# Inverting 32x32 blocks unit by unit, with the rows dealt to four partitions

## The chip, the cores and the metric

The kernel runs on one core of a Trainium2 chip. The metric is the device time of one execution in microseconds (us). "Before" and "after" are the two kernels. Every run lists the span of its profiled execution and the mean granted clock of TensorE. Runs that were timed in rounds are compared with runs of the kernel before on the same chip in the same session; their fast runs lie within about 1.2% of each other for before and 0.4% for the others. Runs of different sessions and chips are also set side by side below; the median of before in these sessions lies between 980.35 and 985.25 us, so a difference of a few microseconds between two sessions means little.

Names of engines: PE is TensorE (PEld its weight loads), DVE VectorE, ACT ScalarE, POOL GpSimd, SP SyncE, which issues transfers.

## The reference, cut to what matters

```python
# q, k, v: (4, 8, 768, 48), beta: (4, 8, 768); w_in: (384, 2048), w_out: (2048, 384), float64
k_n = k / (np.linalg.norm(k, axis=-1, keepdims=True) + 1e-06)
for t in range(S):                       # a recurrence over 768 positions
    y[t]  = q[t] . state
    state = state + beta[t] * outer(k_n[t], v[t] - state . k_n[t])
x = y as (3072 tokens, 384)
h = x @ w_in
out = (h * np.cos(h)) @ w_out            # the FFN
```

The kernels take 64 positions of two batch entries (16 heads) as one **unit**; there are 24 units. Inside a unit the recurrence is a triangular system, whose 64x64 matrices are inverted by halves: two 32x32 triangular blocks by elimination on GpSimd, the rest by matmuls.

## The kernel before

A unit passes four stages, each a generator whose parts are merged with those of other units: `prepare` (norm of k, transposes, Gram matrix), `invert`, `complete` (the other half of the inverse) and `recur` (the recurrence); every two units feed one pass of `ffn`.

```python
def prepare(n):
    nc.scalar.square(ksq, kd)
    nc.vector.tensor_reduce(out=ksum, in_=ksq, ...)
    nc.gpsimd.tensor_tensor(out=knrm, in0=ksum, in1=halves, op=ALU.pow)
    nc.vector.tensor_scalar_add(knrm, knrm, 1e-6)
    nc.vector.reciprocal(krec, knrm)
    nc.gpsimd.tensor_tensor(out=kd, in0=kd, in1=krec..., op=ALU.mult)
    yield
    # ... transposes p_t, copied to kq_t by ScalarE; then the Gram matrix p_g
    nc.scalar.copy(by_parity(g), p_g[:, :, :, 0])
    nc.sync.dma_start(out=g_dr, in_=g)            # through DRAM into gb,
    # ... four units of a group side by side in gb's 128 partitions
    yield

def invert(gr):                                   # four units at once, 6 times
    nc.gpsimd.tensor_tensor(out=a, in0=a, in1=bb[...], op=ALU.mult)   # beta
    # ... clear y, write the diagonal
    for j in range(HC - 1):                       # 31 steps
        shape = [128, j + 1, HC - 1 - j]
        nc.gpsimd.tensor_tensor(out=part, in0=y[:, 0:j+1, j, None]..., in1=a[:, j, None, j+1:]..., op=ALU.mult)
        nc.gpsimd.tensor_tensor(out=behind, in0=behind, in1=part, op=ALU.subtract)
        if j % 5 == 4:
            yield
    nc.sync.dma_start(out=y_drs[gr], in_=yb)      # out to DRAM; complete() reads it back as yt
    yield

def ffn(p):
    for f in range(0, FT, 2):
        # p_h = w_in . x                          TensorE
        # turns <- p_h (ScalarE); r (VectorE, twice); abs, sin of r (ScalarE, twice)
        nc.vector.tensor_tensor(out=gs[-1]..., in0=r, in1=p_h, op=ALU.mult)   # g_ffn
        yield
```

The float64 weights are narrowed to float32 in the kernel, by eight VectorE passes and one GpSimd addition per tile (28 tiles), merged into the first steps.

## Time and profile before

| | before |
|---|---|
| time, median of the first 3 runs | 984.12 us (983.04 to 989.65) |
| span of the profiled run, granted clock | 985.7 us, 0.955 |
| TensorE busy | 775.6 us (79%) |
| VectorE, ScalarE, GpSimd busy | 418.8, 288.7, 336.7 us |
| first 188 us: TensorE busy | 50.1 us |
| units 4 to 20 | 34.2 us per unit, 28.0 to 32.9 in undisturbed steps |

The table reads like this: TensorE has the most work and is idle mainly in two places, the beginning and the six times when GpSimd inverts four units. The prediction below shows the lines.

### The profile page before, as it was taken

To read this page: it belongs to the slowest core of one execution; us is meant where nothing else is said; L and a number is where in the kernel's file an instruction comes from. 1 tells how busy PE (TensorE), PEld (TensorE's weight loads), DVE (VectorE), ACT (ScalarE), POOL (GpSimd) and SP (SyncE) were. 2 spreads that over 40 slices of the span, in tenths; PEclk is the share of its full clock that TensorE was granted. 3 is DMA by queue.
4 is the path that set the end of the run, shared out by engine and by line. 5 is a ranking of instruction groups with operands and counts; after the bars stand their busy time and mean duration, and the time that the engine had idled before them with its cause. 6 is when DMAs were issued, how large, how long until landed. Compare 5 with 4: busy or idle time off the path is not lost. (4 is left out here: it accounts for less than half of the span.)

```text
span 985.7 us, 19148 instructions
## 1 busy us (share of the span) xinstructions
PE 775.6 (79%) x8136; PEld 568.0 (58%) x8136; DVE 418.8 (42%) x772; ACT 288.7 (29%) x530; POOL 336.7 (34%) x481
## 2 busy tenths in 40 slices
PE   0600026729699996899997999988999979999997
PEld 0400025627377674577674686665776847768674
DVE  2586796564235153053262152342441622605141
ACT  1300002124135242044251163341442512515241
POOL 4459734248600159210188011295001850000000
PEclk9999999779799998899998899998999998999999
DMA  6461351540221220231321222303312021000000
GB/s 129 98 191 49 103 130 52 120 88 2 80 51 42 53 55 9 76 66 26 69 40 33 66 53 62 71 2 84 66 25 60 10 78 39 4 18 2 9 9 16
DMA packets 140950, 55.05 MB, mean 56 GB/s; under 512 B 130113, under 2 KB 133441, under 8 KB 140097
## 3 DMA queue, kind: packets, MB, share of 16 engines
q1 hardware_dynamic: 139968, 53.73, 22.5%
q8 instruction: 64, 1.05, 0.5%
q10 hardware_dynamic: 896, 0.10, 0.1%
q14 instruction: 22, 0.17, 0.1%
HBM read 36.41 MB, written 17.40 MB: 55 GB/s over the span
## 5 line engine op out<-in xcount | busy, mean ns | idle before, releaser
L500 PE MATMUL p_o<-w_out,g_ffn 128*128 128x384 f32 x768 | 292.9, 521 | 13.9 <-DVE g_ffn L492 13.3
L471 PE MATMUL p_h<-x_ffn,w_in 128*128 128x256 f32 x1152 | 276.2, 388 | 24.4 <-DVE g_ffn L492 24.2
L471 PEld LDWEIGHTS p_h<-x_ffn,w_in 128*128 128x128 f32 x1152 | 215.4, 192 | 65.5 <-DVE g_ffn L492 17.9
L500 PEld LDWEIGHTS p_o<-w_out,g_ffn 128*128 128x128 f32 x768 | 144.3, 199 | 100.0 <-DVE g_ffn L492 16.8
L243 POOL TENSOR_TENSOR knrm<-ksum,halves 128x8 f32<-128x8 f32 x24 | 40.7, 1697 | 252.9 <-DVE ksum L239 241.2
L328 POOL TENSOR_TENSOR yb<-yb,part 128x31 f32<-128x31 f32 (+15 forms) x186 | 111.1, 597 | 14.0
L492 DVE TENSOR_TENSOR g_ffn<-r,p_h 128x512 f32<-128x512 f32 x96 | 65.8, 685 | 113.8 <-ACT r L489 113.8
L321 POOL TENSOR_TENSOR part<-yb,gb 128x31 f32<-128x31 f32 (+15 forms) x186 | 103.0, 554 | 13.8
L488 ACT ACTIVATE r<-r 128x512 f32<-128x512 f32 x96 | 60.7, 632 | 160.4 <-DVE r L485 160.4
L357 PE MATMUL p_w<-yt,gc 64*64 64x32 f32 x768 | 33.0, 230 | 87.5 <-DMA yt<-y_dr 87.3
L482 DVE SCALAR_TENSOR_TENSOR r<-turns,p_h 128x512 f32<-128x512 int32 x96 | 65.7, 684 | 82.5 <-ACT turns L480 81.8
L357 PEld LDWEIGHTS p_w<-yt,gc 64*64 64x64 f32 x768 | 29.7, 147 | 98.9 <-DMA yt<-y_dr 76.2
L485 DVE SCALAR_TENSOR_TENSOR r<-turns,r 128x512 f32<-128x512 int32 x96 | 75.4, 786 | 2.3
L480 ACT ACTIVATE turns<-p_h 128x512 int32<-128x512 f32 x96 | 57.0, 594 | 61.2 <-PE p_h L471 51.1
L489 ACT ACTIVATE r<-r,halfpi 128x512 f32<-128x512 f32 x96 | 69.5, 724 | 2.6
L279 DVE TENSOR_TENSOR tt<-p_g,masks 128x256 f32<-128x256 f32 x48 | 18.2, 418 | 86.6 <-ACT gc L276 86.6
L258 ACT COPY kq_t<-p_t 128x512 f32<-128x512 f32 x48 | 28.1, 586 | 69.4 <-PE p_t L257 69.3
L417 PE MATMUL p_u<-rhs,yt 64*64 64x48 f32 x704 | 29.6, 230 | 17.3 <-DVE rhs L406 17.3
L307 POOL TENSOR_TENSOR gb<-gb,bb 128x1024 f32<-128x1024 f32 x6 | 14.4, 2400 | 81.6 <-DMA gb<-g_dr 64.1
L510 ACT COPY o<-p_o 128x384 f32<-128x384 f32 x24 | 11.5, 480 | 102.8 <-PE p_o L500 102.8
L371 PEld LDWEIGHTS p_x<-wt,yq 64*64 64x64 f32 x768 | 26.9, 145 | 24.4 <-DVE wt L361 12.7
L417 PEld LDWEIGHTS p_u<-rhs,yt 64*64 64x64 f32 x704 | 25.7, 143 | 26.4 <-DVE rhs L406 19.5
(61 smaller groups left out, 693.8 us busy)
## 6 DMA issues: line engine op xcount, KB each, us to landing
y_dr<-yb SPq DMA_DIRECT2D x6, 1040.0 KB
pairs<-in_moe_w_in_dram SPq DMA_DIRECT2D x12, 512.0 KB
g_dr<-g SPq DMA_DIRECT2D x24, 256.0 KB
pairs<-in_moe_w_out_dram SPq DMA_DIRECT2D x16, 384.0 KB
yt<-y_dr SPq DMA_DIRECT2D x96, 64.0 KB
kp<-in_k_dram SPq DMA_DIRECT2D x48, 96.0 KB
qp<-in_q_dram SPq DMA_DIRECT2D x48, 96.0 KB
vp<-in_v_dram SPq DMA_DIRECT2D x48, 96.0 KB
```

The costliest lines, as they stand in the source:

```text
L321: nc.gpsimd.tensor_tensor(out=part, in0=y[:, 0 : j + 1, j, None].to_broadcast(shape), in1=a[:, j, None, j + 1 :].to_broadcast(shape), op=A ...
L328: nc.gpsimd.tensor_tensor(out=behind, in0=behind, in1=part, op=ALU.subtract)
L357: nc.tensor.matmul(p_w[half(i), h], gc[half(i), h * HC : h * HC + C], yt[half(i), h, HC:C])
L417: nc.tensor.matmul(p_u[half(i), h], yt[half(i), h], rhs[half(i), h])
L471: nc.tensor.matmul(p_h[:, i], w_in[:, t, (f + i) * 128 : (f + i + 1) * 128], x[:, t], start=(t == 0), stop=(t == KT - 1),)
L480: nc.scalar.activation(turns, p_h, AF.Copy, scale=1.0 / (2.0 * math.pi))
L482: nc.vector.scalar_tensor_tensor(out=r, in0=turns, scalar=-PI2_HI, in1=p_h, op0=ALU.mult, op1=ALU.add)
L485: nc.vector.scalar_tensor_tensor(out=r, in0=turns, scalar=-PI2_LO, in1=r, op0=ALU.mult, op1=ALU.add)
L488: nc.scalar.activation(r, r, AF.Abs)
L489: nc.scalar.activation(r, r, AF.Sin, bias=halfpi, scale=-1.0)
L492: nc.vector.tensor_tensor(out=gs[-1][:, f % 4 : f % 4 + 2], in0=r, in1=p_h, op=ALU.mult)
L500: nc.tensor.matmul(p_o, gs[f // 4][:, f % 4, i * 128 : (i + 1) * 128], w_out[:, f], start=(f == 0), stop=(f == FT - 1),)
```

## The change

Its intent: invert each unit by itself, with a quarter of every block's rows on each of four partitions, so that no four units wait for one long inversion and the first inversion is ready early; take the multiplication by beta off GpSimd by putting it into the evictions of g and u, which then move from ScalarE to VectorE; and narrow the weights with three VectorE passes instead of eight. The core of the diff (cuts marked `...`):

```diff
 def prepare(n):
     ...
-    g = work.tile([128, H, C], FP, name="g", bufs=1)
-    nc.scalar.copy(by_parity(g), p_g[:, :, :, 0])
+    g = work.tile([128, H, C], FP, name="g")
+    for par in range(2):
+        nc.vector.tensor_tensor(out=g[:, par::2], in0=p_g[:, par, :, 0], in1=bt[:, n, par::2, None]..., op=ALU.mult)
     ...
-    nc.sync.dma_start(out=g_dr, in_=g)            # and four reads into a quarter of gb
+    for y in range(4):
+        nc.sync.dma_start(out=g_dr[y]..., in_=g[y * HC : (y + 1) * HC, ...])
+    for y in range(4):                            # each block read to four sets of partitions
+        nc.sync.dma_start(out=gb[n][y * HC : (y + 1) * HC]..., in_=g_dr[y]...[None].to_broadcast([SPLIT, H, HC * HC]))
-def invert(gr):
-    nc.gpsimd.tensor_tensor(out=a, in0=a, in1=bb[...], op=ALU.mult)
-    nc.gpsimd.memset(y, 0.0)
+def invert(n):
+    buf = zb[n % 2]
+    nc.scalar.copy(z, eye)                        # the identity, dealt to four partitions
     for j in range(HC - 1):
-        shape = [128, j + 1, HC - 1 - j]
+        rows = j // SPLIT + 1
+        shape = [128, rows, HC - 1 - j]
         ... the same multiply and subtract on GpSimd
-    nc.sync.dma_start(out=y_drs[gr], in_=yb)
+    for y in range(4):
+        nc.sync.dma_start(out=z_drs[n][y]..., in_=buf[y * HC : (y + 1) * HC, ...])
 def recur(n):
-    nc.scalar.copy(u, p_u)
+    nc.vector.tensor_tensor(out=u, in0=p_u, in1=bt[:, n, :, None]..., op=ALU.mult)
 def narrow(dst, src, n):
-    ... eight VectorE passes, one GpSimd addition
+    nc.scalar.activation(t1.bitcast(FP), hi.bitcast(FP), AF.Abs)
+    ... three VectorE passes
+    nc.scalar.activation(t2, lo, AF.Copy, scale=2.0**-29)
+    nc.gpsimd.tensor_tensor(out=w, in0=w, in1=t2, op=ALU.add)
 # step n of the main loop
+    prepare(n + 3), complete(n + 1), recur(n), invert(n + 2), ffn((n - 2) // 2) by halves
```

The norm (knrm and the product kp) stays on GpSimd, as before.

Names used below: g is the Gram matrix times beta, g_dr its copy in DRAM, and gb that copy spread over the partitions for the inversion. zb is the inverse in the making; it goes through z_dr in DRAM to yt, and yq is yt transposed. ksq, ksum, knrm and kp lead from k to its normalised form. Names with p_ are results of matmuls; each lies in a bank, one of the kernel's few buffers for results, and TensorE writes the next one there only when other engines have read it (mostly copying it out, an eviction; in after p_h waits 57.5 us in all for g_ffn). turns, r, g_ffn, p_h and p_o belong to the FFN.

## The prediction

> **What bounds the kernel now.** I read the page first, then the chain of waits in order of time, then stretches of the span, then the times at which one per-unit instruction recurs, then GpSimd by shape. First the page:
>
> ```profile
> span 985.7 us, 19148 instructions
> PE 775.6 (79%) x8136; PEld 568.0 (58%) x8136; DVE 418.8 (42%) x772; ACT 288.7 (29%) x530; POOL 336.7 (34%) x481
> PE   0600026729699996899997999988999979999997
> POOL 4459734248600159210188011295001850000000
> PEclk9999999779799998899998899998999998999999
> ```
>
> TensorE has the work, but not evenly. Its slices are almost empty for the first seven (some 190 us), and later each dip (0, 6, 7) follows a burst of GpSimd (88, 295, 185): the block inversion, done for four units at once. The stretches say the same in us (PE, PEld, DVE, ACT, POOL busy; granted clock; DMA share; GB/s):
>
> ```profile
> 0.00:188.00 188.00, 50.09 (x652) 41.22 (x652) 124.95 (x248) 22.53 (x50) 100.70 (x121) 0.98 0.44 112
> 188.00:280.00 92.00, 66.38 (x675) 47.99 (x674) 39.81 (x76) 23.04 (x40) 51.90 (x76) 0.82 0.21 51
> 345.00:420.00 75.00, 62.49 (x618) 44.76 (x618) 24.74 (x43) 19.73 (x34) 43.33 (x69) 0.89 0.20 46
> 500.00:560.00 60.00, 51.55 (x448) 34.47 (x447) 18.49 (x33) 14.62 (x26) 37.34 (x59) 0.89 0.14 38
> 850.00:936.00 86.00, 86.00 (x833) 61.09 (x832) 27.25 (x47) 27.43 (x46) 0.00 (x0) 1.00 0.03 8
> ```
>
> In the first 188 us TensorE is busy 50; VectorE has 125 and GpSimd 101. Around each group boundary TensorE is idle 8 to 26 us and its clock falls to 0.82 to 0.89; at 850 to 936, with nothing to invert, it is full and at 1.00. How a boundary stalls, in the chain:
>
> ```profile
> 750.80 3.27 issue
> 754.67 2.01 DMA g_dr<-g
> 757.82 2.42 DMA gb<-g_dr
> 760.44 2.36 POOL gb L307
> 802.93 4.35 DMA y_dr<-yb
> 807.72 2.00 DMA yt<-y_dr
> 809.86 0.39 PE p_w L357 x2
> ```
>
> From 760.4 to 802.6 there is only GpSimd (62 multiply and subtract instructions, 39.7 us); then a transfer out, one in, and p_w of the first unit. Four units wait for this one end. What an undisturbed unit costs I take from the starts of the matmuls p_kq (one group per unit):
>
> ```profile
> 283.78 1.15 PE L396 MATMUL p_kq<-st,kq_t 48*64 48x48 f32 x64
> 316.72 1.15 PE L396 MATMUL p_kq<-st,kq_t 48*64 48x48 f32 x64
> 423.53 1.15 PE L396 MATMUL p_kq<-st,kq_t 48*64 48x48 f32 x64
> 562.44 1.15 PE L396 MATMUL p_kq<-st,kq_t 48*64 48x48 f32 x64
> 697.25 1.15 PE L396 MATMUL p_kq<-st,kq_t 48*64 48x48 f32 x64
> ```
>
> These are units 4, 5, 8, 12 and 16; unit 20 starts at 830.3 and unit 23 at 914.0 in the chain. Units 4 to 20 take 546.5 us for 16: 34.2 each. Clean steps are 32.9 with two prepares in the step (283.8 to 316.7) and 28.0 with none (830.3 to 914.0 is 83.7 for 3). So a prepare costs 2.4 and a step with one prepare is 30.4 us.
>
> [...] The trace: 31 elements take 0.25 us and 255 take 0.66 in quiet places, 1.83 ns per element and 0.19 us fixed; start to start there is 0.075 more. So small instructions are mostly fixed cost. [...] among subtracts of 0.6 us single ones take 1.0, eight such within the 40 us above. [...] 0.82 in the stretch with 25.6 us of idle, 1.00 in full ones. [...] the trace has 0.42 us for a tensor_scalar over 512 words and 0.69 for two-input ones.
>
> **The change part by part.**
>
> GpSimd. Before: per group 62 instructions on sum((j+1)(31-j)) = 5456 elements for each of the two kinds; 62 x 0.19 + 2 x 5456 x 0.00183 = 31.8 us clean, 35.7 measured (214.1 busy / 6), 39.7 with gaps. After: a block's 32 rows lie on four partitions, so step j covers j//4+1 rows; the sum is 1560. Clean 62 x 0.19 + 2 x 1560 x 0.00183 = 17.5; gaps 62 x 0.075 = 4.7; contention some 2.5 (eight events of 0.35 in 40 us, scaled to a step of 30). That is about 25 us per unit, 24 times: 600 us in place of 6 x 41. The elements fall by 3.5 per inversion but the instructions are four times as many in all. The beta product (6 x 2.40) and the clearing (6 x 0.96) leave GpSimd. With knrm 1.7, kp 0.9 and the VectorE gap between them 0.7, GpSimd has 28.3 us per step against TensorE's 30.4: it keeps up, with 2 us to spare.
>
> Order. Unit n+2 is inverted in step n and completed in step n+1. GpSimd is in order, so knrm of the next prepare waits behind the inversion, and TensorE meets p_t of that prepare a quarter into its step: the slack is some 5 us, not a whole step.
>
> Narrowing. The eight VectorE passes cost 18.3+13.8+13.0+12.3+22.2+20.7+18.8+16.8 = 135.9 us. After there are three: (0.47+0.59+0.89) x 12 + (0.47+0.61+0.62) x 16 = 51 us. ScalarE gets 28 x 2 x 0.6 = 34 us, in a stretch where it is 12% busy. GpSimd's add stays (37 us).
>
> Evictions with beta. g and u move from ScalarE (0.58, 0.48) to VectorE (2 x 0.42, about 0.5). VectorE then has per step 4 x 2.16 of FFN and about 6 of the rest, half of 30.4. u now queues behind g_ffn, perhaps 1 us later; rhs has always done so and hardly made TensorE wait after 280 except at boundaries.
>
> Transfers. The 128 B pieces move from the read of gb to the write of g_dr, the 256 B pieces from the read of yt to the write of z_dr: the same number per unit. gb grows from 128 to 512 KB per unit, 9 MB more of 55 at an average DMA share of 22%. No gain or loss.
>
> The beginning. The 16 beta transfers hold ScalarE's queue to 12.9 us; four now end near 3. My estimate: first k at 5, knrm to 8, kp at 9.5, two transposes and p_g by 16, g by 18, through DRAM (two trips of about 4, with the weights beside them) by 27; the weight adds ahead on GpSimd make it 30. Inversion 0: 22 + 5 adds of 1.4 = 28 (to 58). Inversion 1: 3.3 + 23 + adds 8.3 = 35 (to 93). Inversions 2 and 3: 3.3 + 23 + 4.2 each (to 124 and 154). The FFN begins in step 2, whose p_t needs inversion 3 done plus 3.3: 157. That point is a quarter into the step, so p_kq of unit 2 starts near 151 and unit 4's at 151 + 60.8 = 212, in place of 283.8: gain 72.
>
> The middle. Units 4 to 20: 16 x 30.4 = 486 in place of 546.5: gain 60. Units 20 to 23: 30.4 + 28 + 28 = 86.4 in place of 83.7: loss 2.7. From 914.0 to the end, 71.7, is the same work. Sum: 985.7 - 72 - 60 + 2.7 = 856 of span; the timed median lies 1.6 under the span: **855 us**.
>
> **The rivals.** (a) GpSimd becomes the bound: 1536 more instructions in its chain, four times as many as before, and 28.3 against 30.4 is a thin margin. If an instruction costs 0.05 more than I take, the step is 31.4 and the time some 875; at 33 us, inversion 23 ends at 154 + 20 x 33 = 814, its p_kq comes some 20 later, and 72 more make 906. For: the fixed cost dominates and contention now meets every step. Against: the measured small instructions (0.25 to 0.33). (b) The start is bound by transfers: g_dr sits behind up to eight weight loads of 512 KB instead of five, on one queue. The DMA share is 0.44 in the first 188 us, which speaks against, but first landings of 10 to 20 us more would give 865 to 875. (c) The middle gains nothing because TensorE waits for VectorE instead: u, g and FFN in one line. Against: 42% busy, and full TensorE at 850 to 936. Each microsecond of stall per unit would add 20: 875. (d) Better than I think: if the inversions start at 22 and the adds hide, 835.
>
> **Range and chances.** The sum is 855. Rivals (a) to (c) each pull by about 20 and are not exclusive; (d) pulls by 20 the other way. I take 828 to 888. To be within 2% of before all of the middle and most of the beginning would have to fail: 3%; slower 2%; faster 95%.
>
> **What would show it.** Right: p_w for the first time near 65 instead of 124; p_kq of unit 4 near 212; even steps of 30 to 31 with granted clock near 1.00 and no dips in the slices; GpSimd at 60 to 70% with an inversion of 62 instructions in 22 to 26 us; VectorE down by some 60 in all. Wrong: p_t or knrm waiting for GpSimd in every step (a); gb landing after 40 (b); p_s waiting for u (c); steps of 33 or more.

0.82 and 1.00 are granted clocks. The "contention" of 2.5 us is the estimate from eight slow instructions in the inversion from 762.9 to 802.9 (five subtracts, three multiplies: 0.71 to 1.22 us, where their neighbours of like size take 0.37 to 0.72). Each of them ran while VectorE made its second pass over r (L485); what slows them, no run shows. And "in order": in after the power to knrm, its input ready at 519.1, starts at 528.14, when the inversion ahead of it has ended.

## More of the kernel before

Where one execution only was made ("one look"), its state is unknown, and only differences of many microseconds are read from it.

## The result, and the profile after

After takes 1073.95 us, median of 4 runs (1071.79 to 1074.3), beside 983.58 of before (978.35 to 989.65, 4 runs). The ratio is 1.0912, 95% interval 1.0847 to 1.0977: 9% slower. (Ratios here are the mean time of one kernel's fast runs over that of the other's in the same rounds, so not quite the quotient of the medians.) The result is correct.

The page of after, the lines that answer to those of before:

```profile
span 1072.4 us, 20510 instructions
PE 811.3 (76%) x8184; PEld 598.7 (56%) x8184; DVE 356.6 (33%) x706; ACT 300.7 (28%) x562; POOL 531.7 (50%) x1579
PE   4123156579797697698698697698697996998998
POOL 3686767675354644644644644644644553460000
PEclk9999997688898898898898898898898998998999
```

The deep dips of before are gone, but a shallow one comes back in every third slice: TensorE never fills, and its clock stays at 0.8 to 0.9 (0.909 in the mean of the span). GpSimd has no bursts and is about half busy in the middle. Nothing is full. The stretches (columns: PE, PEld, DVE, ACT, POOL busy; granted clock; DMA share; GB/s):

```profile
345.00:420.00 75.00, 60.27 (x614) 43.78 (x613) 24.80 (x51) 21.41 (x40) 39.96 (x124) 0.87 0.22 48
500.00:560.00 60.00, 50.24 (x571) 38.37 (x570) 22.81 (x43) 20.26 (x36) 31.34 (x99) 0.91 0.22 50
850.00:936.00 86.00, 76.17 (x821) 55.30 (x820) 30.03 (x56) 24.52 (x47) 37.20 (x125) 0.92 0.20 46
```

In the last of them before had 86.00 of 86.00 at full clock. In after TensorE has 76.17. So the loss shows as waiting, everywhere alike; a smaller part, as the pair of steps below shows, is that matmuls take longer where the granted clock is lower. I put the starts of p_kq, the first recurrence matmul of a unit, side by side (us from the span's start, from the timelines; the kernels of the last three columns come below):

```
unit      before   predicted   after    e6     e13    e15
2            197         151     146   157     141    119
4            284         212     255   260     237    217
5            317         242     305   291     268    254
20           830         698     902   748     725    711
23           914         785     999   832     809    795
span         986         856    1072   905     880    867
4 to 20     34.2        30.4    40.4  30.5    30.5    30.9  per unit
```

After loses 43 us against the prediction by unit 4, 160 from unit 4 to 20 (16 times 10), 11 to unit 23 and 1 behind it: with rounding 216, the whole of 1072 - 856. Most steps alternate between 38 and 42 us.

**One pair of steps.** From the timeline of after (start, duration, engine, line, operation; in brackets the idle time of the engine before it and what ended it). The inversion that began at 504.26 ends at 528.2; this is what stands around its end:

```profile
518.55 0.55 DVE L253 TENSOR_REDUCE ksum<-ksq 128x8 f32<-128x384 f32 x1
519.33 0.72 ACT L508 ACTIVATE r<-r,halfpi 128x512 f32<-128x512 f32 x1
527.98 0.21 POOL L345 TENSOR_TENSOR zb<-zb,part 128x8 f32<-128x8 f32 x1
528.14 1.64 POOL L257 TENSOR_TENSOR knrm<-ksum,halves 128x8 f32<-128x8 f32 x1
529.81 0.17 DVE L258 TENSOR_SCALAR knrm<-knrm 128x8 f32<-128x8 f32 x1 [10.72 <-POOL knrm L257]
530.14 0.64 DVE L511 TENSOR_TENSOR g_ffn<-r,p_h 128x512 f32<-128x512 f32 x1
530.44 0.83 POOL L261 TENSOR_TENSOR kp<-kp,krec 128x384 f32<-128x384 f32 x1 [0.66 <-issue]
530.92 4.38 PE L490 MATMUL p_h<-x_ffn,w_in 128*128 128x256 f32 x12 [9.76 <-DVE g_ffn L511]
535.23 0.88 PE L280 MATMUL p_g<-kq_t 48*64 48x128 f32 x22
537.95 1.78 SPq L308 DMA_DIRECT2D g_dr<-g  x4
539.78 4.03 SPq L314 DMA_DIRECT2D gb<-g_dr  x4
547.55 0.24 POOL L338 TENSOR_TENSOR part<-zb,gb 128x31 f32<-128x31 f32 x1 [16.28 <-DMA gb<-g_dr]
```

Read it along the chain. The norm of a coming unit (ksum) is ready at 519.1, but its power stands behind the inversion on GpSimd and is done at 529.8. VectorE has the addition to it (L258) next in its queue and stops for 10.7 us. Behind it in the same queue is g_ffn, whose input r was ready at 520.05; TensorE's next p_h needs the bank that g_ffn reads and stops for 9.8 us. Behind that p_h in TensorE's queue are 22 of the matmuls p_g of the *next unit to be inverted*, and only they lead to g, g_dr and gb. So GpSimd, free since 531.3, waits 16.3 us for a block whose making it had held up itself. A ring.

VectorE stops here for a norm that nobody needs yet. It is the 17th of the 24 powers, so that of unit 16, and it runs behind the inversion of unit 12; in the order of emission it would stand behind that of unit 14. TensorE's transposes of this unit start 100 us later:

```profile
630.20 0.60 PE L271 MATMUL p_t<-ident,kp 128*128 128x128 f32 x4
```

In this trace, then, VectorE runs its queue in order: g_ffn waits 10 us with its inputs there.

The other step of the pair, at the end of the next inversion (it ends at 569.66):

```profile
569.45 0.21 POOL L345 TENSOR_TENSOR zb<-zb,part 128x8 f32<-128x8 f32 x1
569.69 1.82 SPq L352 DMA_DIRECT2D z_dr<-zb  x4
573.04 0.40 ACT L330 COPY zb<-eye 128x256 f32<-128x256 f32 x1 [10.02 <-DMA z_dr<-zb]
573.88 1.85 SPq L308 DMA_DIRECT2D g_dr<-g  x4
574.36 0.52 ACT L251 ACTIVATE ksq<-kp 128x384 f32<-128x384 f32 x1 [0.91 <-DMA kp<-in_k_dram]
574.79 0.46 ACT L479 COPY x_ffn<-p_z 128x384 f32<-128x384 f32 x1
575.30 1.92 PE L388 MATMUL p_x<-wt,yq 64*64 64x32 f32 x32 [5.28 <-ACT x_ffn L479]
576.25 2.79 SPq L314 DMA_DIRECT2D gb<-g_dr  x4
584.30 0.24 POOL L338 TENSOR_TENSOR part<-zb,gb 128x31 f32<-128x31 f32 x1 [5.19 <-DMA gb<-g_dr]
```

Here it is ScalarE. Its copy of the identity into zb, for the inversion that begins at 628.8, needs the buffer that the transfer z_dr is reading, and that transfer waits for the inversion's end. ScalarE stops for 10 us; x_ffn, behind it, holds TensorE's p_x for 5.3 (p_x takes the bank that x_ffn reads). On SyncE the issue of z_dr waits for the inversion too, and g_dr of the next unit is issued behind it (and behind a load and the read of yt) at 573.9. This costs 4 us: g itself was ready only at 569.7, because TensorE, which had run without a gap since 530.9, came to its p_g at 567.8. Over the whole run SyncE's queue waits 331.4 us for the ends of inversions. The waits of after (columns: total us, times, longest):

```profile
POOL part L338 <- DMA gb<-g_dr: 177.5, 17, 18.0
DVE knrm L258 <- POOL knrm L257: 132.6, 15, 16.3
ACT zb L330 <- DMA z_dr<-zb: 94.9, 11, 14.2
PE p_h L490 <- DVE g_ffn L511: 57.5, 11, 9.8
PE p_x L388 <- ACT x_ffn L479: 52.8, 10, 8.0
SPq L352 <- POOL zb L345: 331.4, 24, 28.1
```

The six lines are the ring: GpSimd waits for gb in 17 of 24 inversions, and VectorE, ScalarE and SyncE wait for GpSimd. Two units take from 504.26 to 584.30, that is 80 us: inversions of 23.9 and 22.1 us, and 19.4 and 14.6 us from the end of one to the begin of the next. On TensorE the same pair (p_kq at 503.35 to p_kq at 584.18) takes some 20 us more than the 61 of two steps in e6 below. Its two stops, 9.8 and 5.3, are 15 of them; the rest is matmuls that take longer after a stop (twelve p_h 4.38 us, elsewhere 2.86; six p_o 4.21, in e6 2.10; the granted clock is 0.62 from 528 to 536 and 0.51 from 575 to 582, and 1.00 from 503.35 to 515 and from 536 to 570).

### The profile page after: what moved, and what is told of

It is laid out like the page before. It is cut to its first block, busy times and chain, and to the rows that moved or that the text cites. A ratio compares the mean times of both kernels' runs of the same rounds, so it can differ in the third digit from the quotient of the medians.

```text
span 1072.4 us, 20510 instructions
## 1 busy us (share of the span) xinstructions
PE 811.3 (76%) x8184; PEld 598.7 (56%) x8184; DVE 356.6 (33%) x706; ACT 300.7 (28%) x562; POOL 531.7 (50%) x1579
## 5 line engine op out<-in xcount | busy, mean ns | idle before, releaser
L490 PE MATMUL p_h<-x_ffn,w_in 128*128 128x256 f32 x1152 | 299.2, 415 | 57.5 <-DVE g_ffn L511 57.5
L338 POOL TENSOR_TENSOR part<-zb,gb 128x60 f32<-128x60 f32 (+24 forms) x744 | 217.3, 292 | 250.5 <-DMA gb<-g_dr 177.5
L490 PEld LDWEIGHTS p_h<-x_ffn,w_in 128*128 128x128 f32 x1152 | 233.9, 209 | 104.0 <-issue 61.8
L519 PE MATMUL p_o<-w_out,g_ffn 128*128 128x384 f32 x768 | 285.1, 520 | 0.6 <-ACT o L529 0.6
L345 POOL TENSOR_TENSOR zb<-zb,part 128x60 f32<-128x60 f32 (+24 forms) x744 | 223.1, 300 | 58.0
L388 PE MATMUL p_x<-wt,yq 64*64 64x32 f32 x768 | 36.0, 254 | 53.7 <-ACT x_ffn L479 52.8
L388 PEld LDWEIGHTS p_x<-wt,yq 64*64 64x64 f32 x768 | 32.9, 174 | 64.7 <-ACT x_ffn L479 59.1
L504 DVE SCALAR_TENSOR_TENSOR r<-turns,r 128x512 f32<-128x512 int32 x96 | 66.6, 696 | 1.4
L258 DVE TENSOR_SCALAR knrm<-knrm 128x8 f32<-128x8 f32 x24 | 4.2, 173 | 132.6 <-POOL knrm L257 132.6
L287 DVE TENSOR_TENSOR g<-p_g,bt 128x256 f32<-128x256 f32 x48 | 18.9, 419 | 82.7 <-PE p_g L280 82.2
L271 PE MATMUL p_t<-ident,kp 128*128 128x128 f32 x96 | 17.5, 313 | 34.2 <-POOL kp L261 31.7
```

Source lines behind the costliest of these rows:

```text
L338: nc.gpsimd.tensor_tensor(out=part, in0=z[:, 0:rows, j, None].to_broadcast(shape), in1=a[:, j, None, j + 1 :].to_broadcast(shape), op=ALU. ...
L388: nc.tensor.matmul(p_x[half(i), h], yq[half(i), h], wt[half(i), h])
L490: nc.tensor.matmul(p_h[:, i], w_in[:, t, (f + i) * 128 : (f + i + 1) * 128], x[:, t], start=(t == 0), stop=(t == KT - 1),)
L504: nc.vector.scalar_tensor_tensor(out=r, in0=turns, scalar=-PI2_LO, in1=r, op0=ALU.mult, op1=ALU.add)
L519: nc.tensor.matmul(p_o, gs[f // 4][:, f % 4, i * 128 : (i + 1) * 128], w_out[:, f], start=(f == 0), stop=(f == FT - 1),)
```

## The experiments

The theories, by the letters that the expectations use. **R**: the ring just read; instructions that wait for the end of an inversion stand in the queues of VectorE (the norm), ScalarE (the copy to zb) and SyncE (the transfer z_dr) ahead of work that TensorE needs. **G**, a rival: GpSimd is simply the bound, its 62 small instructions per unit and all it adds being too much. **V**, another: the evictions of g and u, now on VectorE with beta, hold TensorE up. Where the expectations from e13 on name S, T, S2 and U, those concern the start alone and are told there; in e5 S is another theory, told there.

### Cutting the links, one by one

**e1**: the norm off GpSimd. An inverse square root by a shift and three Newton steps, and the product, all on VectorE.

```diff
-nc.gpsimd.tensor_tensor(out=knrm, in0=ksum, in1=halves, op=ALU.pow)
-nc.vector.tensor_scalar_add(knrm, knrm, 1e-6)
-nc.vector.reciprocal(krec, knrm)
-nc.gpsimd.tensor_tensor(out=kd, in0=kd, in1=krec..., op=ALU.mult)
+... 13 small VectorE instructions that make krec from ksum
+nc.vector.tensor_tensor(out=kd, in0=kd, in1=krec..., op=ALU.mult)
```

> The whole change, with the norm of k (the power and the product with kp) taken from GpSimd to VectorE: a reciprocal square root by shift and three Newton steps on 128x8, some 13 small instructions of 0.2 us. Theory R (a ring of queues: every second unit VectorE's queue stops at the knrm add, which waits for knrm, which stands on GpSimd behind the whole inversion; g_ffn, p_h, p_g, g and gb stand behind it): the waits of 8 to 10 us of p_h for g_ffn go away (57 us in all), also the 16 us at the start; 960 to 1010 us. Rival G (GpSimd's throughput bounds the unit): GpSimd loses 2.5 us per unit, so at most 60 us come off, and inversions then run back to back. Rival V (evictions with beta on VectorE cost it): VectorE has 2 us more per unit, so the same or slower.

Measured (one look): 1025.33 us, 49 less than after (1073.95). The steps alternate between 31 and 44 to 47: one of two is as clean as predicted, the other longer than the 42 of after. The waits show where the rest went:

```profile
POOL part L355 <- DMA gb<-g_dr: 248.1, 17, 23.2
ACT zb L347 <- DMA z_dr<-zb: 139.5, 18, 15.0
```

The wait of VectorE for knrm is gone, and ScalarE's wait for z_dr rose from 94.9 to 139.5. One link is cut and the ring closes over the next. R had expected 960 to 1010 and missed; G had allowed up to 60 less, so this run doesn't part the two.

**e2**: the copy to zb emitted as before, but tied behind the copy of gc of its own unit (a zero read from p_g is its bias), so that it cannot go ahead of that unit's evictions.

```diff
+nc.scalar.activation(zero[n], p_g[:, 1, NP - 1, 0, HC : HC + 1], AF.Copy, scale=0.0)
-nc.scalar.copy(z, eye)
+nc.scalar.activation(z, eye, AF.Identity, bias=zero.pop(n))
```

> The whole change, but the copy that sets zb to the identity on ScalarE is tied (by a zero bias made in the prepare of its own unit) to stand behind gc of its own unit, not a unit earlier. Theory R: in every other unit ScalarE's queue stops at this copy until z_dr of the running inversion has landed (94.9 us in 11 waits), with x_ffn behind it and p_x behind that (52.8 us): these waits vanish, 1010 to 1045 us. Rivals G and V: nothing on GpSimd or VectorE changes, so within 1% of 1074.

Measured (one look): 1081.68, that is 8 more than after. R missed here (1010 to 1045), and the number is what G and V expected. Alone this link is worth nothing; GpSimd still waits 180.2 us for gb and VectorE 135.3 for knrm.

**e3**: the transfer z_dr issued by GpSimd, which has just ended the inversion, in place of SyncE.

```diff
-            nc.sync.dma_start(out=z_drs[n][y]..., in_=buf[...])
+            nc.gpsimd.dma_start(out=z_drs[n][y]..., in_=buf[...])
```

> The whole change, with z_dr written from GpSimd's own queue instead of SyncE's. Theory R: SyncE no longer stops for the end of the inversion (331 us), so g_dr and gb of the next unit, which in every second unit stand behind z_dr, go out while the inversion still runs; the wait of GpSimd for gb falls from 16 to some 5 us in those units; 1000 to 1050 us, less if the other two links of the ring hold the same time. Rival G: GpSimd gets 4 descriptor jobs more per unit, so the same or slower (1074 to 1110).

Measured (one look): 1055.14, 19 less. Steps of 35 to 37 and 44. GpSimd's 96 issues of z_dr take 57.6 us (0.60 each). VectorE's wait for knrm rose from 132.6 to 205.2 us: again the next link. R missed by 5 us, and G expected no gain. The three single cuts, then, don't settle it.

**e4**: the three together.

> All three together: no queue but GpSimd's own waits for the inversion before it has to. Theory R: units of 30 to 31 us, TensorE full, 850 to 890 us, faster than the kernel before. Rival G: GpSimd still has 24 us of inversion and its gaps, so units stay near 40 and the time above 1000. Rival V: g, u and the norm on VectorE keep the units at 35 or more, above 950.

Measured (3 rounds): 967.92 us (966.68 to 969.71), ratio to before 0.984 (0.9791 to 0.9889). That is 106 less than after, where the single cuts had given 49, -8 and 19, in sum 60. The ranges of R (850 to 890) and of G (above 1000) both missed; V's "above 950" was met, and falls with e6 and e8. The links are not costs to be added but alternatives: here the ring ran as fast as its slowest remaining link let it. Steps of 30.2 and 38 to 41 are left; in the long ones a fourth link holds. VectorE's transpose yq, which waits for yt and so for an inversion's end, stands ahead of g (from the timeline of e4):

```profile
518.21 0.71 DVE L390 STREAM_TRANSPOSE yq<-yt 128x512 f32<-128x512 f32 x1 [12.09 <-DMA yt<-z_dr]
518.85 0.72 DVE L304 TENSOR_TENSOR g<-p_g,bt 128x256 f32<-128x256 f32 x2
```

VectorE waits 12 us for yt (170.8 us in 18 waits over the whole run), and only then makes the g that the next inversion starts from.

**e5**: one unit more of lookahead, on after alone. Prepare is four units ahead, invert three, so that the inversion's result is needed a whole step later.

```diff
-KEEP = 4
+KEEP = 5                # and a third buffer in DRAM, one for ksq
-    prepare(n + 3) ... invert(n + 2)
+    prepare(n + 4) ... invert(n + 3)
-NARROW = {-3: 4, -2: 5, -1: 7, 0: 4, 1: 4, 2: 4}
+NARROW = {-4: 4, -3: 5, -2: 7, -1: 4, 0: 4, 1: 4}
```

> The whole change with prepare and inversion one unit earlier (prepare n+4 and invert n+3 in step n; one more buffer where needed), queues else as they are. Theory R as refined (what stops a queue is an instruction that needs the inversion's result or follows it on GpSimd and that was put into the queue too early): knrm, the copy to zb and z_dr keep their places against the inversion, so only yq and yt get slack; two units stay at 74 to 81 us, 1000 to 1075 us in all. Rival S (there was simply one unit too little of slack, whatever the queues): units near 31, about 860 us. Rival G: near 1074.

Measured (one look): 1075.58, the same as after within 2 us; steps of 39.4 to 41.2. Rival S of this expectation (one unit too little of slack, and nothing else) is out. A step more of slack doesn't help, since the norm, the zb copy and z_dr wait for the inversion itself, not for its use: VectorE still waits 145.1 us for knrm and ScalarE 76.2 for z_dr. It can only free yq, which isn't the link that holds here.

**e6**: e4 with e5's lookahead.

> The three changes of e4_all and the unit earlier of e5_look together. In e4_all the units alternate 30 and 39 to 41 us, and in the long ones the chain runs from the end of the inversion over z_dr, yt and yq to g, which stands behind yq in VectorE's queue, then g_dr and gb, to the next inversion. Theory R: with the inversion a unit earlier yq never waits; units of 30 to 31.5 us, 865 to 905 us. Rival G: GpSimd's 24 us of inversion, 2.3 us of descriptors and contention bound it; units stay at 35, about 965.

Measured (3 rounds): **908.14 us** (907.36 to 909.07), ratio to before 0.9239 (0.9186 to 0.9292), correct; 60 less than e4. Its page, and one of the stretches shown above:

```profile
PE   3210154367999999999999999999999999999997
PEclk9999999587999999999999999999999999999999
```

```profile
500.00:560.00 60.00, 60.00 (x687) 44.15 (x685) 30.65 (x74) 22.71 (x44) 41.24 (x129) 1.00 0.30 66
```

(The 908 us are 3 above the range that R expected; what is missing lies in the start.) From about unit 4 on TensorE is busy without a gap, at full clock, in steps of 30.2 and 30.8. The prediction had 30.4. For the same 8184 matmuls its busy time is 756.2 us, beside 811.3 in after. GpSimd does all its inversions in this kernel (41 us of 60, with the issues of z_dr: 96 of 64 KB in the whole run, 56.0 us, 0.58 each) and holds nothing up. Rival G is out.

### Leaving one cut out

If the links are alternatives, putting any one back into e6 should bring the ring back. **e9** is e6 with the norm on GpSimd again, **e10** with the unbound copy to zb, **e11** with z_dr on SyncE (each edit the reverse of those above).

> e6_look_all without its first part: the norm of k goes back to GpSimd, behind the inversions. Theory R, where each queue that stops for an inversion is enough to close the ring: VectorE's knrm add stops again and g_ffn behind it, long units of 40 or more come back in every second step, 970 to 1040 us. If only the sum of the work on GpSimd mattered: 2.5 us more per unit on an engine that is 60% busy, 905 to 925 us.

> e6_look_all without its second part: the copy to zb may again stand early in ScalarE's queue (in the compiled order ahead of ksq and x_ffn in every second unit). Theory R: it is the weakest link (alone it gave nothing), yet x_ffn waits for z_dr again in every second unit: 915 to 960 us. If it does not matter once the inversions come a unit earlier: 903 to 912 us.

> e6_look_all without its third part: z_dr is again written from SyncE's queue, which stops until the inversion ends, with g_dr and gb of the next unit behind it in every second unit. Theory R: GpSimd then waits 14 us for gb after each such inversion (24 + 14 = 38 and 30 in turn): 940 to 990 us. If the unit of slack hides it: 900 to 912 us (GpSimd is spared 2.3 us of descriptors per unit).

Measured (one look each): 1009.32, 1002.94 and 1016.71 us, that is 101, 95 and 109 more than e6. The copy to zb, worth -8 alone, is worth 95 at the end; e10 and e11 lost more than R had expected of them (up to 960 and 990). Steps: 30.2 and 41; 30.8 and 41; 31 and 41 to 44. The wait that was put back is there each time: VectorE for knrm 175.6 us in e9, ScalarE for z_dr 74.1 in e10, SyncE for the inversions' ends 387.4 in e11. Theory R stands: each link alone brings back more than half of the loss, and none of them is a cost of its own.

### The parts of the change that the ring hides

**e8**: are the evictions on VectorE to blame? g and u are copied by ScalarE as before; beta is left out, so the result is wrong (relative error 2.49).

```diff
-        nc.vector.tensor_tensor(out=g[:, par::2], in0=p_g[:, par, :, 0], in1=bt..., op=ALU.mult)
+nc.scalar.copy(by_parity(g), p_g[:, :, :, 0])
-nc.vector.tensor_tensor(out=u, in0=p_u, in1=bt..., op=ALU.mult)
+nc.scalar.copy(u, p_u)
```

> The whole change with g and u copied out by ScalarE as before and without beta, so a wrong result on purpose. Rival V (VectorE's two evictions cost the time): 950 to 1030 us. Theory R: the queues stop for the inversion as before, 1055 to 1090 us.

Measured (one look): 1092.93, 19 more than after (why more, no run shows). Rival V is out: the evictions gain nothing by going back, and e6 has its clean steps with them on VectorE.

**e7**: before with the new narrowing alone.

> The kernel before with the new narrowing alone. VectorE loses some 85 us of work in the first 190; the first FFN starts earlier by perhaps 15 to 30 us (between the first p_w at 124 and the first p_h at 189 VectorE was the busy engine), the rest stays: 955 to 975 us. If the start is bound elsewhere (the one long inversion to 116): no change beyond 5 us.

Measured (3 rounds): 962.68 us (961.97 to 963.84), ratio to before 0.9797 (0.973 to 0.9865). Unit 4 starts at 265 instead of 284. So this part of the change is worth some 20 us by itself; in after the loss of the middle outweighs it.

### The start

In e6 all that is missing from the predicted 855 lies ahead of unit 4 (260 against 212). **e12** deals the narrowing otherwise over the first steps, to have less of it where the first inversions are:

```diff
-NARROW = {-4: 4, -3: 5, -2: 7, -1: 4, 0: 4, 1: 4}
+NARROW = {-4: 3, -3: 3, -2: 3, -1: 3, 0: 4, 1: 6, 2: 6}
```

> e6_look_all with the narrowing of the weights spread over more steps (3,3,3,3,4,6,6 in place of 4,5,7,4,4,4), so that fewer of GpSimd's weight adds stand ahead of the first inversions. The steps are clean after 260 us in e6_look_all, so only the start can move: if the adds ahead of the inversions set it, 5 to 20 us less, 888 to 903; if the transfers or the inversions themselves do, within 4 us of 908.

Measured (3 rounds): 916.63 us (916.05 to 917.72), ratio 0.9304 (0.9275 to 0.9332): 8 more than e6, outside both branches of the expectation. Unit 2 starts 10 us earlier and unit 4 even 28 (232), but unit 5 10 us later (301): moving the work about doesn't remove what it waits for. Among the waits in e6's first 270 us are:

```profile
DVE t L215 <- ACT t L214: 64.9, 10, 15.6
ACT t L225 <- POOL w_in L226: 38.4, 7, 11.1
ACT t L225 <- POOL w_out L226: 22.7, 5, 7.7
```

The new narrowing has its own such ring: GpSimd's additions of the low bits stand between the inversions; ScalarE's copies (L225) wait for them to free one of two buffers; VectorE's passes wait for ScalarE. (The copy to zb waits in this stretch too, 43.0 us in 5 waits; e15 comes to it.) **e13** joins the low bits by one VectorE instruction, which truncates the weights where the kernel was written to round them (the result is still correct against the reference); **e14** gives the copies four buffers of their own. Theory **S**: the additions and the copies behind them hold the start up; its rival **T**: transfers or VectorE's work do.

```diff
 # e13, from e6
-nc.scalar.activation(t2, lo, AF.Copy, scale=2.0**-29)
-nc.gpsimd.tensor_tensor(out=w, in0=w, in1=t2, op=ALU.add)
+nc.vector.scalar_tensor_tensor(out=w, in0=lo, scalar=29, in1=w, op0=ALU.logical_shift_right, op1=ALU.bitwise_or)
 # e14, from e6 (input buffers of the weights, which g_ffn shares, 6 instead of 8, for room)
-t2 = ffn_pool.tile([128, 2 * TOK], U32, name="t2", tag="r")[:, 0:n]
+t2 = ffn_pool.tile([128, 2 * TOK], U32, name="t2", bufs=4)[:, 0:n]
```

> The version with all four links cut (908.1 us), with the weights' low bits joined by one VectorE instruction (shift right by 29, then OR: truncation instead of rounding) in place of ScalarE's copy and GpSimd's addition. Theory S: at the start, GpSimd's additions stand between the inversions and ScalarE's copies wait for their buffer, so ScalarE and VectorE stop for GpSimd and the FFN starts some 50 us late; without them unit 4 starts some 20 to 45 us before 260 and the time is 865 to 890. Rival T: the start is set by the weights' transfers or by VectorE's own work, to which this adds 28 instructions; then unit 4 stays at 255 to 265 and the time is within 5 us of 908, or longer.

> The version with all four links cut (908.1 us), the copies' low bits in four buffers of their own instead of two shared ones (the weights' input buffers 6 instead of 8 to make room). Theory S in its narrow form (only the buffer wait of ScalarE's copy stops the start): 890 to 903 us, and that wait gone from the list of waits. Wide form (GpSimd's additions come late whatever the buffers): within 5 us of 908. Rival T: within 5 us of 908, or longer for want of input buffers.

Measured (3 rounds each): e13 882.05 us (881.1 to 882.37), ratio 0.8978 (0.8939 to 0.9018), unit 4 at 237; e14 902.44 (901.85 to 903.55), ratio 0.9191 (0.9143 to 0.924), unit 4 at 255. S holds and T falls: 26 us go with the additions, though VectorE does more. With the buffers alone it is 6 (and unit 4 starts 5 earlier): the copies' waits for GpSimd are gone from the list of waits, but ScalarE's waits for zb rise from 43.0 to 64.8 us.

In e13 unit 2 starts at 141, earlier than predicted, but from there to unit 4 it takes 96 us in place of 61. The timeline shows one old link again:

```profile
153.67 0.51 ACT L352 ACTIVATE zb<-eye,zero 128x256 f32<-128x256 f32 x1 [10.52 <-DMA z_dr<-zb]
154.08 0.57 ACT L290 COPY kq_t<-p_t 128x512 f32<-128x512 f32 x1
154.70 1.12 PE L289 MATMUL p_t<-ident,qp 128*128 128x128 f32 x4 [9.57 <-ACT kq_t L290]
```

While the first inversions follow each other without a pause, the copy to zb waits for the transfer of two units before, and TensorE's transposes stand behind it. **e15** gives e13 three zb buffers (and seven weight buffers, for room), **e16** gives e14 the same (with three t2 buffers). Theory **S2** is this wait; rival **U** is TensorE's own lower clock (in e13 0.66 from 141 to 176 and 0.86 to 200) and the order of its work.

```diff
-zb = [const.tile([128, HC + ROWS * PITCH], FP, name=f"zb{i}") for i in range(2)]
+zb = [const.tile([128, HC + ROWS * PITCH], FP, name=f"zb{i}") for i in range(3)]
-    buf = zb[n % 2]
+    buf = zb[n % 3]
```

> e13 (882.1 us) with three buffers zb instead of two, so that ScalarE's copy of the identity does not wait for the transfer out of the inversion two units before (to make room, seven weight buffers instead of eight). In e13's start that copy waits 6.4, 10.5 and up to 18 us, and the kq_t copy that TensorE needs stands behind it (TensorE waits 9.6 at 154.7). Theory S2 (this ring is what is left of the start): unit 4 starts 10 to 20 us before 237 and the time is 860 to 874. Rival U (what is left is TensorE's own work at a lower clock, 73 us busy between units 2 and 4, and the order of FFN work): within 4 us of 882.

> e14 (902.4 us), which rounds the weights as the kernel after does, with three buffers zb (and three instead of four for the copies' low bits). Theory S2: 880 to 895. Rival U: within 4 us of 902.

Measured (3 rounds each): e15 **869.4 us** (868.32 to 871.61), ratio 0.8878 (0.886 to 0.8897), unit 2 at 119, unit 4 at 217, correct; e16 898.38 (898.1 to 898.71), ratio 0.9171 (0.9156 to 0.9187). In e15 S2 holds, with 13 us (10 by the ratios to before, since the chips differ). In e16, where the additions are still there, it gives 4 by the medians, within noise by the ratios: less than S2 expected and what U did. It looks like another link that counts only when the one ahead of it is cut. e15 is the fastest version, 11% under before; e16 is the fastest that is written to round the weights, as both kernels are.

What is left of e15's distance from the prediction is 11 us of span (867 against 856), all of it by unit 5 (254 against 242). TensorE is granted 0.79 of its clock from 120 to 200; how much of the 12 us that explains, no run here takes apart.

## Why the prediction was wrong, point by point

**The step that failed** is the paragraph "Order": "the slack is some 5 us, not a whole step", and with it the sentence before, "it keeps up, with 2 us to spare". It counted GpSimd's busy time per step (28.3 us) against TensorE's (30.4) and took the 5 us as the distance between two fixed schedules. The wait that it looked for, TensorE's p_t for the norm, came only four times, all in the first 58 us (31.7 us); since the norms run ahead of their order of emission, the wait that came was VectorE's, at the addition to knrm (132.6 us, 15 times). And the start of an inversion isn't free: it hangs on g, g_dr and gb, and these stand, in the queues of VectorE, TensorE and SyncE, behind instructions that wait for the end of the inversion before. The quantity to compare with 30.4 is therefore not the busy time but the way round the ring: an inversion of 22 to 24 us, plus some 17 us from its end through knrm, g_ffn, p_h and p_g, or through z_dr and g_dr, to the landing of gb. That is 40 us, which is what the steps measure (40.4), and 16 steps of 10 us are the 160 us lost in the middle. The "Middle" term, a gain of 60, became a loss of 100 (646.5 against 546.5). That the three links and the lookahead together bring it to 488, and that each of the links put back costs 95 to 109 us, is shown by e6 and e9 to e11.

**The beginning.** "That point is a quarter into the step, so p_kq of unit 2 starts near 151" held in the number (145.8), by luck: it was worked out from the end of inversion 3 at 154, and that inversion only began at 146.9 and ended at 169.7. TensorE did not wait for it, because the norm that p_t of this step needs (unit 5) had run at 136.6, behind inversion 2. "Unit 4's at 151 + 60.8" failed: from unit 2 to 4 it took 109.6 us. The 60.8 are two undisturbed steps; in the beginning there were none. Cutting the links of the middle doesn't mend it (unit 4 at 260 in e6); taking away the additions of the narrowing and then the buffer wait of the copy to zb, both behind inversions, brings it to 237 (e13) and 217 (e15).

**The rivals as put.** (a) "GpSimd becomes the bound": its steps of 33 us and its thin margin did not come about; e6 has the same inversions at 30.5 us a step. The mark that was to show it, "p_t or knrm waiting for GpSimd in every step", was half there (132.6 us of waits for knrm in 15 of 24 units, p_t hardly), and would have misled: it shows a queue, not a full engine. (b) Transfers at the start: no sign; gb had landed by 35.8, when the first inversion began. (The first p_w came at 74.4, predicted near 65.) (c) VectorE's evictions: refuted by e8 and e6. None of the rivals was a cycle through several engines, and the range, which let rivals add up by 20 us each, had no room for one.

**What was right.** The inversion: 62 instructions in 22.1 (547.55 to 569.66) and 23.9 us, predicted 22 to 26. (Its 744 multiplications, of 8 to 76 elements, took 292 ns in the mean over the run, beside the 0.19 us that the prediction took as fixed.) The clean step, 30.4: e6 has 30.5. VectorE's busy time: down 62.2 (418.8 to 356.6), predicted 60. From unit 23 to the end: 73.1, predicted 71.7. The narrowing: a gain, of some 20 us alone (e7). (One reading was loose: of the "almost empty" first seven slices of before, two are at 6.)

**A term of the wrong size.** "No gain or loss" for the transfers. The read of gb, now 512 KB in place of 128 per unit, ends 3.7 and 5.3 us after its last issue in the two steps above (543.81 to 547.55, 579.04 to 584.30), where the chain of before has 2.42 for its last transfer. Off the path this would cost nothing, but it lies on the ring; no run takes its share apart.

## What to carry to other kernels

When a long operation on one engine is dealt out unit by unit, compare the period not with its busy time but with the whole way round: from its end, through every queue that has something waiting for it, back to the data that starts the next one (here 40.4 us per unit with no engine above 76%, and 30.5 in e6 with the waits elsewhere). Read the order of the queues from the trace, not from the order in which the program emits. List, for each engine, which instruction waits for the long operation and what stands behind it; move those waits to the engine that did the work, or late in the queue, or give them another buffer. Cut all the links before judging any: one by one these were worth 49, -8 and 19 us, together 106, and with one step of lookahead 166.
